# Small rows of w_up on four DMA loads of 8, 10, 12 and 14 engines

## The chip, the cores and the metric

The kernel runs on one core of a Trainium2 chip (trn2). The metric is the time of one execution in microseconds (us) of device time; lower is better. The first six runs of the kernel before agree within 0.3% (80.38 to 80.61 us). Some executions are over 1.5% slower than the fastest of their kernel; these are called slow and are left out of every comparison here, medians included. Two kernels, x8 and x14, were run once for their traces alone, so their state isn't known. In the profiles PE is TensorE (PEld its loads of weights), DVE is VectorE, ACT ScalarE, and SP the engine whose queue issues the loads. Because single traces matter in this study, each number says from which run it is.

## The reference, cut to what matters

One token is decoded: attention over a window of 4096 keys (part A) and a gated unit (part B), mixed by a gate. The change touches only `w_up`.

```python
def _B_ref(x, w_gate, w_up, w_down):          # x: 1x1x512, F = 1792
    g = jnp.einsum("bsd,df->bsf", x, w_gate)
    u = jnp.einsum("bsd,df->bsf", x, w_up)
    h = _sigmoid(g) * u
    return jnp.einsum("bsf,fd->bsd", h, w_down)
# ... a = attention(x, k_cache, v_cache, wq, wo)
return g * a + (1 - g) * b
```

All weights and caches together are 30.7 MB, each byte read once (the page of the kernel before counts 30.67 MB read), so the kernel is a stream of loads with the arithmetic beside it.

## The kernel before

All large loads are issued by SP in one order: wq, four of K (`kn`), w_gate, the main part of w_up, the small rows of w_up (`wx_sb`), four of V (`vv`), wo, w_down. A large load has 128 partitions and runs on all 16 DMA engines (busy share 1.00 of 16 from 60 to 69 us). A partition holds four rows of w_up; the last of the four, less its first 448 columns, is split off: 128 small rows of 1344 elements (2,688 bytes). They land in 64 partitions, in two slots `h`, by four loads of 32 rows:

```python
    wx_sb = const.tile([64, 2, FX], BF16, name="wx_sb")
    wx_v = B_w_up.rearrange("(h b j i c) f -> h b i j c f", h=2, b=2, j=4, i=8)[:, :, :, :, DC - 1, F - FX:F]
    for h in range(2):
        for b in range(2):
            dq.dma_start(wx_sb[32 * b:32 * b + 32, h, :], wx_v[h, b])
    # ... (cut) vv, wo, w_down
    spare = const.tile([1, 1], F32, name="spare")
    for _ in range(4):
        nc.vector.memset(spare[:], 0.0)
    # ... (cut) the same order of rows for x: xp, xx
    # in the second GLU, for the last quarter c == DC - 1 and j >= 1:
                    for h in range(2):
                        nc.tensor.matmul(g_out, lhsT=xx[:, h:h + 1].to_broadcast([64, 32]),
                                         rhs=wx_sb[:, h, (j - 1) * FQ:j * FQ], start=False, stop=(h == 1))
```

In the trace eight of 16 streams carry the rows, 16 each: no more than eight rows are under way at once, and each of the four loads counts eight completions. The other eight streams carry none of them. The trace has no engine numbers; the text calls the eight engines 0 to 7 and the others 8 to 15, as the description of the change does. It doesn't show either which partitions an engine writes. Where the rows land turns out to matter.

Of the kernel before, what the change touches and what calls it, by code (L numbers as in the profile page):

```python
# [12 lines left out]
BF16 = mybir.dt.bfloat16  # L13
F32 = mybir.dt.float32
# [3 lines left out]
def kernel(  # L18
# [14 lines left out]
    nc = tc.nc  # L33

    P = 128
    D = A_x.shape[-1]
    DC = D // P
# [8 lines left out]
    F = B_w_gate.shape[1]  # L46
# [3 lines left out]
    FQ = F // 4  # L50
# [11 lines left out]
    const = ctx.enter_context(tc.tile_pool(name="const", bufs=1))  # L62
# [7 lines left out]
    ps_m = ctx.enter_context(tc.tile_pool(name="ps_m", bufs=2, space=bass.MemoryType.PSUM))  # L70


    xr = const.tile([1, 2, D], BF16, name="xr")
# [3 lines left out]
    dq = nc.sync  # L77
# [11 lines left out]
    for a in range(HP):  # L89
# [7 lines left out]
    FX = 3 * FQ  # L97
    LM = DC * F - FX
    dq.dma_start(wu_sb[:].rearrange("p c f -> p (c f)")[:, 0:LM],
                 B_w_up.rearrange("(p c) f -> p (c f)", c=DC)[:, 0:LM])  # L100
    wx_sb = const.tile([64, 2, FX], BF16, name="wx_sb")
    wx_v = B_w_up.rearrange("(h b j i c) f -> h b i j c f", h=2, b=2, j=4, i=8)[:, :, :, :, DC - 1, F - FX:F]
    for h in range(2):
        for b in range(2):
            dq.dma_start(wx_sb[32 * b:32 * b + 32, h, :], wx_v[h, b])

    vv = []
    for a in range(HP):
# [16 lines left out]
    ident = const.tile([P, P], BF16, name="ident")  # L125
# [7 lines left out]
    nc.gpsimd.tensor_copy(permT[:].rearrange("p (k j) -> p k j", j=4),  # L133
                          ident[:].rearrange("p (j k) -> p k j", j=4))
    spare = const.tile([1, 1], F32, name="spare")
    for _ in range(4):
        nc.vector.memset(spare[:], 0.0)

    other = const.tile([2, HQ * 4 // R2, 2, REP], BF16, name="other")
# [7 lines left out]
    for c in range(DC):  # L147
        nc.tensor.matmul(xt_ps[:, c:c + 1], lhsT=xr[:, 0, c:D:DC], rhs=ident[0:1, 0:1],  # L148
                         start=True, stop=True, skip_group_check=True)
    xx_ps = ps_m.tile([64, 2], F32, name="xx_ps", tag="m")  # L150
    xp = const.tile([1, 2, 64], BF16, name="xp")
    for h in range(2):
        nc.vector.tensor_copy(xp[:, h, :].rearrange("o (b i j) -> o b i j", b=2, j=4),
                              xr[:, 0, :].rearrange("o (h b j i c) -> o h b i j c", h=2, b=2, j=4, i=8)[:, h, :, :, :, DC - 1])
        nc.tensor.matmul(xx_ps[:, h:h + 1], lhsT=xp[:, h, :], rhs=ident[0:1, 0:1],
                         start=True, stop=True, skip_group_check=True)
    xT = const.tile([P, DC], BF16, name="xT")
    nc.vector.tensor_copy(xT[:], xt_ps[:])
    xx = const.tile([64, 2], BF16, name="xx")
    nc.vector.tensor_copy(xx[:], xx_ps[:])  # L160


# [18 lines left out]
    for u in range(4):  # L181
        nc.tensor.matmul(S_ps[u // 2][:, u % 2, :], lhsT=other[:].rearrange("p o y u -> p (o y u)"),  # L182
                         rhs=ident[0:2, 0:2].rearrange("p (o y) -> p o y", o=1).to_broadcast([2, 256, 2]),
                         start=True, stop=False)
# [11 lines left out]
    for k in range(8):  # L196
        q_ps = ps_big.tile([P, 512], F32, name="q_ps", tag="b")
        ks = slice(k * 512, (k + 1) * 512)
        for c in range(DC):
            nc.tensor.matmul(q_ps[:], lhsT=xT[:, c:c + 1].to_broadcast([P, P]),  # L200
                             rhs=wq_sb[:, c, ks], start=(c == 0), stop=(c == DC - 1))
# [18 lines left out]
    for a in range(HP):  # L220
        for v in range(2):
            kT = kTs[a, v] if (a, v) in kTs else k_transpose(a, v)
            k_v = kT[:].rearrange("p (n dhi s t) -> p n dhi s t", n=KB, dhi=2, s=32)
            for dhi in range(2):
                for t in range(2):
                    for hb in range(2):
                        nc.tensor.matmul(S_ps[v][:, hb, :], lhsT=q_st[:, a, dhi, :, t],  # L227
                                         rhs=k_v[:, hb * 16:(hb + 1) * 16, dhi, :, t],
                                         start=False, stop=(a == HP - 1 and dhi == 1 and t == 1))
# [4 lines left out]
    def glu(w, wsb):  # L234
        for c in range(DC):
            for j in range(4):
                g_out = gu_ps[w][32 * j:32 * j + 32, 0:FQ]
                if w == 1 and c == DC - 1 and j >= 1:
                    for h in range(2):
                        nc.tensor.matmul(g_out, lhsT=xx[:, h:h + 1].to_broadcast([64, 32]),  # L240
                                         rhs=wx_sb[:, h, (j - 1) * FQ:j * FQ], start=False, stop=(h == 1))
                    continue
                nc.tensor.matmul(g_out, lhsT=xT[:, c:c + 1].to_broadcast([P, 32]),  # L243
                                 rhs=wsb[:, c, j * FQ:(j + 1) * FQ], start=(c == 0), stop=(c == DC - 1))


    pm2 = work.tile([P, 2], F32, name="pm2")
    for v in range(2):
        nc.vector.tensor_reduce(pm2[:, v:v + 1], S_ps[v][:].rearrange("p a b -> p (a b)"), axis=AX.X, op=ALU.max)  # L249
    pm = work.tile([P, 1], F32, name="pm")  # L250
    nc.vector.tensor_tensor(pm[:], pm2[:, 0:1], pm2[:, 1:2], op=ALU.max)
    glu(0, wg_sb)
    sge = work.tile([P, FQ], F32, name="sge")
    nc.scalar.activation(sge[:], gu_ps[0][:, 0:FQ], AF.Exp, scale=-1.0)  # L254
# [7 lines left out]
                     start=True, stop=True)  # L262
# [34 lines left out]
    for a in range(HP):  # L297
        for m in range(NP // 4):
            nc.tensor.matmul(pv_ps[32 * a:32 * a + 32, :, :],  # L299
                             lhsT=eT[:, a, 4 * m:4 * m + 4, :].rearrange("p n r -> p (n r)"),  # L300
                             rhs=vv[a][:, 4 * m:4 * m + 4, :],
                             start=(m == 0), stop=(m == NP // 4 - 1))
# [7 lines left out]


    glu(1, wu_sb)

    o_ps = ps_m.tile([P, HQ], F32, name="o_ps", tag="m")
# [59 lines left out]
```

## Time and profile before

| | before |
|---|---|
| time, median of the first 3 runs | 80.46 us (80.45 to 80.61) |
| span of the core in the profile | 78.7 us |
| share of the chain that ended last | DMA 93% |
| rate of the loads, 30 to 39 us | 426 GB/s |
| last completion count of w_down | 75.84 us |

The chain of waits tells what the end waited for, step by step. The windows tell how busy the 16 DMA engines are in a stretch. The records of single DMA packets, of which these views are made, hold start, length and size; where this document speaks of streams, every packet was linked to the one that ends where it starts, which gives one stream for each engine. "Landing" is the time at which an engine's count arrives at the semaphore of a load.

### The profile page before, as it was taken

What the parts mean: (1) busy time and instruction counts of PE and PEld (TensorE: products, weight loads), DVE (VectorE), ACT (ScalarE), POOL (GpSimd) and SP (SyncE); (2) the same over time, 40 slices, a digit from 0 to 9 for tenths busy, and PEclk for the clock granted to TensorE, in tenths of its full rate; (3) what the DMA queues carried; (4) which work ended last, traced back from release to release, by engine and by line L of the source; (5) the groups of instructions that cost most, each with busy time, mean ns of one, the idle gap of its engine ahead of it and who ended that gap; (6) DMA issues with size and microseconds to landing.
All of it is one profiled execution on the core that took longest, in us unless ns stands there. A gap on an engine that the chain in (4) does not pass through costs nothing.

```text
span 78.7 us, 798 instructions
## 1 busy us (share of the span) xinstructions
PE 52.5 (67%) x314; PEld 23.6 (30%) x314; DVE 38.8 (49%) x52; ACT 10.9 (14%) x20; POOL 3.3 (4%) x10
## 2 busy tenths in 40 slices
PE   0200094999905788898887307999996799567650
PEld 0200041344302333333332202344341345345420
DVE  1600920029869999999986349962000000690020
ACT  2400000247651000000002191000000002000010
POOL 7900000000000000000000000000000000000000
PEclk9999999999999999999999995699999999999997
DMA  7779799999999999999999999999999999999710
GB/s 184 300 316 533 316 483 391 408 425 458 441 408 416 425 474 416 386 437 417 438 410 426 441 416 441 408 433 441 416 433 433 424 425 433 416 391 409 290 42 1
DMA packets 2616, 30.71 MB, mean 390 GB/s; under 512 B 307, under 2 KB 438, under 8 KB 822
## 3 DMA queue, kind: packets, MB, share of 16 engines
q1 hardware_dynamic: 2608, 30.67, 92.9%
q8 instruction: 2, 0.03, 0.2%
q10 hardware_dynamic: 6, 0.00, 0.0%
HBM read 30.67 MB, written 0.00 MB: 390 GB/s over the span
## 4 chain that ended last, share of the span: by engine, by line
DMA 93%; SPq 2%; PE 1%; DVE 1%; issue 0%
DMA wd_sb<-in_B_w_down_dram 36%; DMA kn<-in_A_k_cache_dram 32%; DMA vv<-in_A_v_cache_dram 24%; SPq L84 2%; PE a_ps L290 1%; DVE res L341 1%; SPq L80 0%
## 5 line engine op out<-in xcount | busy, mean ns | idle before, releaser
L299 PE MATMUL pv_ps<-vv,eT 128*32 128x512 bf16 x64 | 15.9, 405 | 4.1 <-DVE eT L271 2.8
L227 PE MATMUL S_ps<-kT,qbig 128*128 128x512 bf16 x64 | 15.2, 378 | 5.0 <-DVE qbig L216 2.8
L188 DVE STREAM_TRANSPOSE kT<-kn 128x2048 f32<-128x2048 f32 x8 | 17.8, 2282 | 0.0
L227 PEld LDWEIGHTS <-qbig 128*128 128x128 bf16 x64 | 6.1, 97 | 14.1 <-issue 4.2
L299 PEld LDWEIGHTS <-eT 128*32 128x32 bf16 x64 | 6.2, 102 | 12.9 <-issue 4.2
L200 PE MATMUL q_ps<-wq_sb,xT 128*128 128x512 bf16 x32 | 8.8, 442 | 1.2 <-DMA wq_sb<-in_A_wq_dram 1.2
L318 DVE TENSOR_TENSOR oT<-o_ps,rb 128x32 bf16<-128x32 f32 x1 | 0.2, 191 | 13.5 <-PE o_ps L316 13.5
L205 DVE STREAM_TRANSPOSE qtT<-q_sb 128x512 f32<-128x512 f32 x4 | 2.7, 700 | 6.9 <-ACT q_sb L202 6.9
L182 PE MATMUL S_ps<-ident,other 2*128 2x512 bf16 x4 | 2.0, 611 | 5.8 <-DVE other L140 5.8
L202 ACT CAST q_sb<-q_ps 128x512 bf16<-128x512 f32 x8 | 4.7, 585 | 7.0 <-PE q_ps L200 7.0
L200 PEld LDWEIGHTS <-xT 128*128 128x128 bf16 x32 | 3.5, 111 | 6.8 <-issue 4.2
L290 PE MATMUL a_ps<-wo_sb,oY 128*1 128x256 bf16 x64 | 3.8, 272 | 1.5 <-DMA wo_sb<-in_A_wo_dram 1.2
L290 PEld LDWEIGHTS <-oY 128*1 128x1 bf16 x64 | 2.7, 83 | 3.1 <-issue 1.4
L271 DVE STREAM_TRANSPOSE eT<-e_sb 128x1024 bf16<-128x1024 bf16 x2 | 2.4, 1224 | 1.9 <-ACT e_sb L269 1.9
L254 ACT ACTIVATE sge<-gu_ps 128x448 f32<-128x448 f32 x1 | 0.5, 543 | 18.9 <-PE gu_ps L243 18.9
L309 ACT COPY pv_sb<-pv_ps 128x512 f32<-128x512 f32 x1 | 0.6, 585 | 17.7 <-PE pv_ps L299 17.7
L341 DVE CAST res<-a_ps 1x256 bf16<-1x256 f32 x1 | 0.4, 412 | 5.2 <-PE a_ps L290 5.2
L281 DVE RECIPROCAL sg<-sge 128x448 f32<-128x448 f32 x1 | 3.0, 2952 | 0.0
L165 DVE TENSOR_TENSOR gpr<-xr 1x512 f32<-1x512 bf16 x1 | 0.7, 679 | 4.6 <-DMA xr<-in_gate_w_dram 4.6
L249 DVE TENSOR_REDUCE pm<-S_ps 128x1 f32<-128x1024 f32 x2 | 2.4, 1208 | 0.9 <-PE S_ps L227 0.9
L290 PE MATMUL a_ps<-wd_sb,hT 128*1 128x256 bf16 x28 | 2.1, 271 | 0.8 <-DMA wd_sb<-in_B_w_down_dram 0.8
L148 PE MATMUL xt_ps<-ident,xr 1*128 1x1 bf16 x4 | 0.3, 165 | 3.5 <-POOL ident L126 3.5
(62 smaller groups left out, 31.0 us busy)
## 6 DMA issues: line engine op xcount, KB each, us to landing
kn<-in_A_k_cache_dram SPq DMA_DIRECT2D x4, 2048.0 KB, 27.2
vv<-in_A_v_cache_dram SPq DMA_DIRECT2D x4, 2048.0 KB, 19.1
wq_sb<-in_A_wq_dram SPq DMA_DIRECT2D x1, 4096.0 KB
wo_sb<-in_A_wo_dram SPq DMA_DIRECT2D x2, 2048.0 KB
wg_sb<-in_B_w_gate_dram SPq DMA_DIRECT2D x1, 1792.0 KB
wu_sb<-in_B_w_up_dram SPq DMA_DIRECT2D x1, 1456.0 KB
wd_sb<-in_B_w_down_dram SPq DMA_DIRECT2D x1, 1024.0 KB
wd_sb<-in_B_w_down_dram SPq DMA_DIRECT2D x1, 384.0 KB
```

Of the source, the lines that this page charges most:

```text
L84: dq.dma_start(t[:, n0:n1, :].rearrange("p n d -> p (n d)"), cache[0, 2 * a:2 * a + 2, SBASE:SBASE + W, :] .rearrange("y (x n) d -> x y n ...
L182: nc.tensor.matmul(S_ps[u // 2][:, u % 2, :], lhsT=other[:].rearrange("p o y u -> p (o y u)"), rhs=ident[0:2, 0:2].rearrange("p (o y) -> p ...
L188: nc.vector.transpose(t[:].bitcast(F32), kn[a][:, v * KB:(v + 1) * KB, :] .rearrange("p n d -> p (n d)").bitcast(F32))
L200: nc.tensor.matmul(q_ps[:], lhsT=xT[:, c:c + 1].to_broadcast([P, P]), rhs=wq_sb[:, c, ks], start=(c == 0), stop=(c == DC - 1))
L202: nc.scalar.copy(q_sb[:, ks], q_ps[:])
L205: nc.vector.transpose(qtT[:].bitcast(F32)[:, kq], q_sb[:].bitcast(F32)[:, kq])
L227: nc.tensor.matmul(S_ps[v][:, hb, :], lhsT=q_st[:, a, dhi, :, t], rhs=k_v[:, hb * 16:(hb + 1) * 16, dhi, :, t], start=False, stop=(a == HP ...
L249: nc.vector.tensor_reduce(pm2[:, v:v + 1], S_ps[v][:].rearrange("p a b -> p (a b)"), axis=AX.X, op=ALU.max)
L271: nc.vector.transpose(eT[:, :, v * KB:(v + 1) * KB, :].rearrange("p a n r -> p n a r"), e_sb[:, v, :].rearrange("p (n a r) -> p n a r", a= ...
L281: nc.vector.reciprocal(sg[:], sge[:])
L290: nc.tensor.matmul(a_ps[32 * i:32 * i + 1, i, 0:HN], lhsT=lhsT, rhs=rhs[:, i * HN:(i + 1) * HN], start=start, stop=stop)
L299: nc.tensor.matmul(pv_ps[32 * a:32 * a + 32, :, :], lhsT=eT[:, a, 4 * m:4 * m + 4, :].rearrange("p n r -> p (n r)"), rhs=vv[a][:, 4 * m:4 ...
```

## The change

Its intent, by the description that came with it: the rows spread over more engines, so that engines 8 to 15 carry 8 to 0 of them and engines 0 to 7 carry 12 instead of 16. The rows land in 128 partitions, one slot. That the kernel's 8, 10, 12 and 14 (`k` in the diff) would be the numbers of engines was an expectation; the trace of the kernel after tests it below.

```diff
-    wx_sb = const.tile([64, 2, FX], BF16, name="wx_sb")
-    wx_v = B_w_up.rearrange("(h b j i c) f -> h b i j c f", h=2, b=2, j=4, i=8)[:, :, :, :, DC - 1, F - FX:F]
-    for h in range(2):
-        for b in range(2):
-            dq.dma_start(wx_sb[32 * b:32 * b + 32, h, :], wx_v[h, b])
+    wx_sb = const.tile([P, FX], BF16, name="wx_sb")
+    WX_PARTS = []
+    for k, r in ((8, 4), (10, 3), (12, 2), (14, 3)):
+        e0 = sum(kk * rr for _, kk, rr in WX_PARTS)
+        WX_PARTS.append((e0, k, r))
+        dq.dma_start(wx_sb[e0:e0 + k * r, :], B_w_up[DC * e0:DC * (e0 + k * r), :]
+                     .rearrange("(j i c) f -> i j c f", j=r, i=k)[:, :, DC - 1, F - FX:F])
...
-    for _ in range(4):
+    for _ in range(2):
         nc.vector.memset(spare[:], 0.0)
... (xp is gathered by four copies instead of two, in the order of the rows; one xx matmul instead of two)
+                xc, rhs = xT[:, c:c + 1], wsb[:, c, j * FQ:(j + 1) * FQ]
                 if w == 1 and c == DC - 1 and j >= 1:
-                    for h in range(2):
-                        nc.tensor.matmul(g_out, lhsT=xx[:, h:h + 1].to_broadcast([64, 32]),
-                                         rhs=wx_sb[:, h, (j - 1) * FQ:j * FQ], start=False, stop=(h == 1))
-                    continue
... (cut)
+                    xc, rhs = xx[:], wx_sb[:, (j - 1) * FQ:j * FQ]
```

More of the change, by code (lines that the diff above doesn't have):

```diff
@@ L149 @@
                          start=True, stop=True, skip_group_check=True)
-    xx_ps = ps_m.tile([64, 2], F32, name="xx_ps", tag="m")
-    xp = const.tile([1, 2, 64], BF16, name="xp")
-    for h in range(2):
-        nc.vector.tensor_copy(xp[:, h, :].rearrange("o (b i j) -> o b i j", b=2, j=4),
-                              xr[:, 0, :].rearrange("o (h b j i c) -> o h b i j c", h=2, b=2, j=4, i=8)[:, h, :, :, :, DC - 1])
-        nc.tensor.matmul(xx_ps[:, h:h + 1], lhsT=xp[:, h, :], rhs=ident[0:1, 0:1],
-                         start=True, stop=True, skip_group_check=True)
+    xx_ps = ps_m.tile([P, 1], F32, name="xx_ps", tag="m")
+    xp = const.tile([1, P], BF16, name="xp")
+    for e0, k, r in WX_PARTS:
+        nc.vector.tensor_copy(xp[:, e0:e0 + k * r].rearrange("o (i j) -> o i j", i=k),
+                              xr[:, 0, DC * e0:DC * (e0 + k * r)].rearrange("o (j i c) -> o i j c", j=r, i=k)[:, :, :, DC - 1])
+    nc.tensor.matmul(xx_ps[:], lhsT=xp[:], rhs=ident[0:1, 0:1], start=True, stop=True)
     xT = const.tile([P, DC], BF16, name="xT")
     nc.vector.tensor_copy(xT[:], xt_ps[:])
-    xx = const.tile([64, 2], BF16, name="xx")
+    xx = const.tile([P, 1], BF16, name="xx")
     nc.vector.tensor_copy(xx[:], xx_ps[:])
@@ L237, in glu @@
                 g_out = gu_ps[w][32 * j:32 * j + 32, 0:FQ]
+                xc, rhs = xT[:, c:c + 1], wsb[:, c, j * FQ:(j + 1) * FQ]
                 if w == 1 and c == DC - 1 and j >= 1:
-                    for h in range(2):
-                        nc.tensor.matmul(g_out, lhsT=xx[:, h:h + 1].to_broadcast([64, 32]),
-                                         rhs=wx_sb[:, h, (j - 1) * FQ:j * FQ], start=False, stop=(h == 1))
-                    continue
-                nc.tensor.matmul(g_out, lhsT=xT[:, c:c + 1].to_broadcast([P, 32]),
-                                 rhs=wsb[:, c, j * FQ:(j + 1) * FQ], start=(c == 0), stop=(c == DC - 1))
+                    xc, rhs = xx[:], wx_sb[:, (j - 1) * FQ:j * FQ]
+                nc.tensor.matmul(g_out, lhsT=xc.to_broadcast([P, 32]), rhs=rhs,
+                                 start=(c == 0), stop=(c == DC - 1))
     pm2 = work.tile([P, 2], F32, name="pm2")
```

## The prediction

> **What bounds the kernel now.** I read the page's chain first. It says that the kernel is one long load:
>
> ```profile
> DMA 93%; SPq 2%; PE 1%; DVE 1%; issue 0%
> DMA wd_sb<-in_B_w_down_dram 36%; DMA kn<-in_A_k_cache_dram 32%; DMA vv<-in_A_v_cache_dram 24%; SPq L84 2%; PE a_ps L290 1%; DVE res L341 1%; SPq L80 0%
> ```
>
> The compute engines hold 1% each. The chain in order of time shows the end: the w_down load lands at 75.51 us, six matmuls and one copy follow.
>
> ```profile
> 46.84 28.67 DMA wd_sb<-in_B_w_down_dram
> 75.51 0.04 issue
> 75.55 0.66 PE a_ps L290 x6
> 76.20 0.40 DVE res L341
> ```
>
> So I ask which DMA engine brings the last piece of w_down. The windows of equal stretches answer half of it (columns: stretch, its length, busy us of PE, PEld, DVE, ACT, POOL, clock, DMA share of 16 engines, GB/s):
>
> ```profile
> 30.00:39.00 9.00, 7.85 (x35) 3.21 (x34) 9.00 (x5) 0.00 (x0) 0.00 (x0) 1.00 1.01 426
> ...
> 60.00:69.00 9.00, 6.91 (x60) 3.47 (x59) 1.40 (x4) 0.58 (x1) 0.00 (x0) 1.00 1.00 426
> ...
> 74.00:74.50 0.50, 0.50 (x12) 0.40 (x10) 0.00 (x0) 0.00 (x0) 0.00 (x0) 1.00 0.64 242
> 74.50:75.00 0.50, 0.50 (x13) 0.31 (x10) 0.00 (x0) 0.00 (x0) 0.00 (x0) 1.00 0.63 229
> 75.00:75.40 0.40, 0.36 (x6) 0.15 (x3) 0.00 (x0) 0.00 (x0) 0.00 (x0) 1.00 0.30 103
> ```
>
> All 16 engines are busy until 69 us, then a share of 0.63 is left, which is 10 of 16: six engines finish about 1.5 us before the other ten. The end is set by the engine with the most to carry, not by the sum of bytes. Why ten? The page's queues name the second kind of traffic:
>
> ```profile
> q1 hardware_dynamic: 2608, 30.67, 92.9%
> q8 instruction: 2, 0.03, 0.2%
> ```
>
> Two packets of instructions, of 16,384 bytes each. In the packet records of the trace I linked every packet to the one that ends where it starts; this gives 16 streams, one for each engine, though it doesn't give the engines' numbers. What the streams show:
> - A packet of 16,384 bytes takes 0.614 us in every stage (26.7 GB/s), alike on all engines. An engine runs at its own rate and never waits for another.
> - Eight streams carry the small rows (2,688 bytes, 16 each, four runs of four with a 4-byte completion after each). One row takes 0.104 us, one run 0.42 us, the four 1.68 us: for one such stream from 39.46 to 41.14 us. The other eight start on vv meanwhile.
> - The instruction packets start at 39.60 and 69.45 us, in two different streams, both of the eight without small rows. Each takes 1.06 and 1.10 us, and the data packet after it takes 1.11 us instead of 0.61 and 0.77 instead of 0.31. A fetch costs its engine 1.55 us.
>
> So the kernel before is balanced already: eight engines pay 1.68 us for small rows, two pay 1.55 us for a fetch, and six pay nothing and end early. At the end of wo, the streams with rows stand at 70.55 to 70.90 us, the one of the first fetch at 70.58, the others at 69.11 to 69.35; the one of these that the second fetch then hits stood at 69.14. From there to the end of w_down an undisturbed stream needs 4.48 us. Last packets are therefore at 75.03 to 75.38 (rows), 75.06 (first fetch), 69.14 + 4.48 + 1.56 = 75.18 (second), 73.6 to 73.8 (six free ones). The records' last packet indeed ends at 75.38; its completion counts 0.46 us later, at 75.84.
>
> [...]
>
> **The change, part by part.**
> *The loads.* (8,4), (10,3), (12,2), (14,3) are k and rows per engine.[...] Rows per engine: 0 to 7 have 4+3+2+3 = 12; 8 and 9 have 3+2+3 = 8; 10 and 11 have 2+3 = 5; 12 and 13 have 3; 14 and 15 none. The sum is 96+16+10+6 = 128, as before; 0.34 MB are moved and none removed. With 0.104 us for a row and 0.006 for a completion, engines 0 to 7 pay 12 x 0.104 + 4 x 0.006 = 1.27 us instead of 1.68, so they end 0.41 us earlier, at 74.62 to 74.97. Engines 8 to 15 pay 0.85, 0.85, 0.53, 0.53, 0.32, 0.32, 0, 0.
> An engine without a fetch then ends at 73.8 + 0.85 = 74.65 at most and isn't last. What matters is the two with a fetch: they stood at 75.06 and 75.18, and keep that or add their rows. The last engine moves from 75.38 to 75.18 (no rows: -0.20 us), to about 75.5 (three rows: +0.1), 75.7 (five: +0.3) or 76.0 (eight: +0.6).
> *Issue.* Four loads remain, each 0.68 to 0.82 us on SP's queue. The last is issued by 23.4 us, while the engines reach them at 39.5 us. Nothing of this is on the path.
> *PE.* In the second GLU three matmuls of 128 rows replace six of 64. The six stand from 65.69 to about 66.25 us, so about 0.28 us less work, and one transposition of x replaces two at the start. PE then waits 1.22 us for wo and 0.8 us for w_down, so this gain is hidden.[...]
> *DVE.* Four small copies for xp instead of two, two dummy memsets instead of four: the count is kept, and DVE waits 4.6 us for gate_w there. Nothing.
>
> **The rivals.**
> (a) *The fetches hit engines 14 and 15, or others without rows.* For it: the gradient looks drawn for this, and both fetches fell on the upper half. Then the last engine gains only 0.2 us, since the fetch engine becomes the bound: 80.25 us.
> (b) *A fetch hits engine 8 or 9.* For it: nothing in the trace says which of the upper eight it is. Against it: the design. The time would be 80.46 + 0.6 = 81.05 us.
> (c) *The full gain of 0.41 us.* It needs fetches that cost nothing, or that end before; the streams at 75.06 and 75.18 speak against it. 80.05 us.
> (d) *A fetch moves to an engine with 12 rows*[...]: 1.27 + 1.55 against 1.68, so +1.1 us, 81.6 us. Against it: four runs of before within 0.22 us of each other suggest that the engine is fixed[...].
> (e) *A wait for PE takes over.* Against: it is ahead of the loads from 66 us on.
>
> **Range and chances.** I can't see the engine numbers, so I weigh by hand: no rows on the worse fetch engine 0.35 (-0.2 us), three rows 0.25 (+0.1), five 0.2 (+0.3), eight 0.2 (+0.6); together +0.13 us. I take 80.5 us. Streams differ in phase by 0.35 us from their start on, which shifts who is last by 0.1 to 0.2 us; with cases (a) to (b) this gives 80.1 to 81.1 us. 2% is 1.6 us; faster by that is out of reach, as all 16 engines' mean end is (8 x 75.2 + 2 x 75.1 + 6 x 73.7)/16 = 74.6, only 0.8 us before the last. Slower by it needs (d) and more.
>
> **What would show it right or wrong.** In the packet records of the changed kernel the streams should carry 12, 8, 5, 3 and 0 rows of 2,688 bytes on eight, two, two, two and two engines, which also tells the number of the fetch's engine up to a pair. The rows' streams should end vv 0.41 us earlier against the free ones. In the last half microsecond before the end the DMA share should fall to one or two sixteenths (0.06 to 0.13) instead of ten, because only fetch engines are left; the last landing of w_down should sit 1.55 us plus rows after a free engine's. It is wrong if the last streams are again those of engines 0 to 7, if a fetch costs other than 1.55 us, or if k comes out otherwise (all rows of a load on one or two engines would cost whole microseconds).

## The result, and the profile after

| | before | after |
|---|---|---|
| median of 6 runs | 80.46 us (80.38 to 80.61) | 81.88 us (81.18 to 83.03), two of them slow |
| fast runs | all six, median 80.46 | 81.18, 81.70, 81.78, 81.98, median 81.74 |
| ratio, fast runs | | 1.0147 (95%: 1.0106 to 1.0187) |

A ratio is the mean time of one kernel's fast runs over that of the other's fast runs of the same rounds, so it isn't quite the ratio of the medians. The change costs 1.5%; the prediction, 80.5 us in a range of 80.1 to 81.1, missed it.

First what came out as worked out. The page's queues of the kernel after (packets, MB, share of 16 engines):

```profile
q1 hardware_dynamic: 2620, 30.67, 91.9%
q8 instruction: 2, 0.03, 0.2%
```

The load queue has 12 packets more than before and the same bytes. That is 8+10+12+14 = 44 completions for the rows instead of 4 x 8 = 32, and at their semaphores the four loads count 8, 10, 12 and 14: they do run on so many engines. And again there are two instruction packets. At the end of the loads, in equal stretches of the kernel after (DMA share and GB/s are the last two columns):

```profile
75.50:76.00 0.50, 0.50 (x10) 0.34 (x6) 0.00 (x0) 0.00 (x0) 0.00 (x0) 0.50 0.13 47
76.00:76.50 0.50, 0.50 (x12) 0.37 (x10) 0.00 (x0) 0.00 (x0) 0.00 (x0) 0.87 0.06 20
```

A share of 0.13, then 0.06: two engines, then one, as the prediction had it for the streams that were hit by a fetch. But they are at it half a microsecond to a microsecond later than was worked out. What was missed lies around 40 us. One stretch from 39 to 43.5 us, in which the rows are read and the first V load begins, before and after:

```profile
39.00:43.50 4.50, 3.54 (x28) 1.25 (x26) 3.49 (x4) 0.54 (x1) 0.00 (x0) 1.00 1.03 426
```

```profile
39.00:43.50 4.50, 4.21 (x32) 1.69 (x30) 3.62 (x3) 0.00 (x0) 0.00 (x0) 1.00 1.03 345
```

The reader should look at the last two columns. Busy share 1.03 in both (the share comes from the packets' lengths, so it can pass 1), but 426 GB/s before and 345 after: the engines are occupied all the time and move a fifth less. (426 - 345)/426 x 4.5 us = 0.86 us are lost, by all 16 engines together. The packet records say the same. Before, all 128 rows take 107 to 112 ns. After, the rows take about 107 ns up to 40.05 us, and from then on, as the third load begins, up to 294 ns (61 of the 128 take over 115 ns); the V packets beside them take up to 1.20 us instead of 0.614. Even the two streams without rows land their first V load at 45.99 and 46.10 us, where an unburdened stream of the kernel before did so at 45.05 to 45.27.

The second part is at the end. The chain of waits in order of time, kernel after:

```profile
42.50 30.09 DMA wo_sb<-in_A_wo_dram
72.58 0.04 issue
72.62 5.15 PE a_ps L289 x60
77.77 0.40 DVE res L340
```

Before, six matmuls followed the last landing. Here the chain leaves the loads at wo and follows PE through its last 60 matmuls. The windows say why; PEclk, third column from the right, is the granted clock of TensorE (before, then after):

```profile
72.70:76.10 3.40, 2.60 (x40) 1.53 (x34) 0.00 (x0) 0.00 (x0) 0.00 (x0) 1.00 0.56 211
```

```profile
72.70:76.10 3.40, 3.40 (x34) 2.21 (x35) 0.00 (x0) 0.00 (x0) 0.00 (x0) 0.50 0.76 295
```

In this execution TensorE was granted half its clock (0.50) from 72.71 to 76.13 us, and PE was busy all through it (3.40 of 3.40 us). The last landing was at 76.87 us, and the output's DMA was issued 1.38 us later; before it was 0.84 us. So the profiled execution's 1.58 us (span 80.32 against 78.74) divide into 76.87 - 75.84 = 1.03 us of later landing and 1.38 - 0.84 = 0.54 us of half-clock tail. Only the first part is in every trace of the kernel after. Its second trace, below, has a full clock in the tail and 81.18 us.

### The profile page after: what moved, and what is told of

Same layout as the page of the kernel before. It is cut to its first block, busy times and chain, and to the rows that moved or that the text cites. A ratio compares the mean times of both kernels' runs of the same rounds, so it can differ in the third digit from the quotient of the medians.

```text
span 80.3 us, 790 instructions
## 1 busy us (share of the span) xinstructions
PE 54.5 (68%) x310; PEld 24.6 (31%) x310; DVE 38.8 (48%) x52; ACT 10.9 (14%) x20; POOL 3.3 (4%) x10
## 4 chain that ended last, share of the span: by engine, by line
DMA 83%; PE 6%; SPq 6%; issue 1%; DVE 0%
DMA wu_sb<-in_B_w_up_dram 46%; DMA wo_sb<-in_A_wo_dram 37%; PE a_ps L289 6%; SPq L84 4%; SPq L94 1%; SPq L117 1%; DVE res L340 0%; SPq L80 0%
## 5 line engine op out<-in xcount | busy, mean ns | idle before, releaser
L228 PE MATMUL S_ps<-kT,qbig 128*128 128x512 bf16 x64 | 16.3, 404 | 3.9 <-DVE qbig L217 2.8
L201 PE MATMUL q_ps<-wq_sb,xT 128*128 128x512 bf16 x32 | 9.4, 466 | 1.6 <-DMA wq_sb<-in_A_wq_dram 1.6
L289 PE MATMUL a_ps<-wo_sb,oY 128*1 128x256 bf16 x64 | 5.4, 343 | 2.5 <-DMA wo_sb<-in_A_wo_dram 2.2
L289 PEld LDWEIGHTS <-oY 128*1 128x1 bf16 x64 | 3.4, 102 | 4.8 <-issue 2.4
L253 ACT ACTIVATE sge<-gu_ps 128x448 f32<-128x448 f32 x1 | 0.5, 544 | 18.9 <-PE gu_ps L242 18.9
L183 PEld LDWEIGHTS <-other 2*128 2x128 bf16 x4 | 0.6, 158 | 6.2 <-DVE other L142 5.9
```

Source lines behind the costliest of these rows:

```text
L183: nc.tensor.matmul(S_ps[u // 2][:, u % 2, :], lhsT=other[:].rearrange("p o y u -> p (o y u)"), rhs=ident[0:2, 0:2].rearrange("p (o y) -> p ...
L201: nc.tensor.matmul(q_ps[:], lhsT=xT[:, c:c + 1].to_broadcast([P, P]), rhs=wq_sb[:, c, ks], start=(c == 0), stop=(c == DC - 1))
L228: nc.tensor.matmul(S_ps[v][:, hb, :], lhsT=q_st[:, a, dhi, :, t], rhs=k_v[:, hb * 16:(hb + 1) * 16, dhi, :, t], start=False, stop=(a == HP ...
L289: nc.tensor.matmul(a_ps[32 * i:32 * i + 1, i, 0:HN], lhsT=lhsT, rhs=rhs[:, i * HN:(i + 1) * HN], start=start, stop=stop)
```

## The experiments

The theory after the first look: **P**, the place: rows are slow because of the partitions in which they land, and the jam spreads to other streams. Behind it stood an assumption of the author about which engine writes which partitions, and that engines slow each other where they write side by side. No trace here shows that; the runs show only what each choice of partitions and of rows for each engine took. Rivals: **R**, the new order of reading rows from memory; **F**, the fetch of instructions, which in the profiled run began at 40.14 us, within 0.1 us of the stall; **G**, rows on more than eight engines stall wherever they land.

All results in one table; the first kernel's profiled trace and the second trace of it (in the row "before") agree within 0.1 us. "Rows" is the sum of the lengths of the 128 row packets, "rate" the stretch 39 to 43.5 us, "landing" the last count of w_down in the trace, "closing" the time from the output's DMA issue to the end of the span.

| kernel | fast runs, us | ratio to before | rows, us | rate, GB/s | landing, us | closing, us |
|---|---|---|---|---|---|---|
| before (traces: first, x8) | 80.31 to 80.71 | 1 | 13.7, 13.7 | 426, 430 | 75.84, 75.91 | 2.05, 2.06 |
| after (traces: first, x4, x11, x14) | 81.11 to 82.18 | 1.015, 1.015, 1.016 | 18.1, 17.5, 18.9, 18.0 | 345, 342, 321, 331 | 76.87, 76.64, 77.63, 76.55 | 2.07, 2.06, 2.06, 2.06 |
| x1_upper | 81.91 to 82.03 | 1.020 | 24.2 | 274 | 77.42 | 2.06 |
| x2_even16 | 81.03 to 81.39 | 1.010 | 13.7 | 431 | 76.33 | 2.24 |
| x3_lower | 81.77 to 82.18 | 1.019 | 22.2 | 294 | 77.20 | 2.29 |
| x5_pairs | 81.17 to 81.76 | 1.013 | 19.5 | 337 | 76.95 | 2.18 |
| x6_shift4 | 80.14 to 80.98 | 1.002 | 14.2 | 403 | 75.57 | 2.29 |
| x7_ten | 80.67 to 81.39 | 1.009 | 15.7 | 405 | 76.28 | 2.02 |
| x9_aligned | 80.95 to 81.39 | 1.009 | 13.7 | 430 | 76.25 | 2.34 |
| x10_best | 80.56 to 81.29 | 1.005 | 13.7 | 416 | 75.70 | 2.28 |
| x12_best64 | 80.23 to 80.64 | 0.9988 | 13.7 | 433 | 75.92 | 2.05 |
| x13_before65 | 80.74 to 81.08 | 1.005 | 13.7 | 426 | 75.93 | 2.28 |

### x1_upper: the old loads into the other half of the partitions

```diff
-            dq.dma_start(wx_sb[32 * b:32 * b + 32, h, :], wx_v[h, b])
+            dq.dma_start(wx_sb[64 + 32 * b:96 + 32 * b, h, :], wx_v[h, b])
... (tile of 128 partitions; xx_ps, xx and the matmuls use partitions 64 to 127)
```

> The kernel before, its four loads of eight engines unchanged, but the rows land in partitions 64 to 127 instead of 0 to 63. Theory P[...]: the rows' packets take well over 107 ns, all engines are held up by 0.9 to 1.7 us around 40 to 42 us as in the changed kernel, the time is 81.3 to 82.2 us. Theory R (reads: the order in which rows are read from memory, or the uneven k, causes the stall) and theory F (the instruction fetch falling among the small rows causes it): nothing changes, 80.4 to 80.6 us, rows at 107 ns.

The same engines read the same rows in the same order; only the partitions differ. The window of its trace:

```profile
39.00:43.50 4.50, 4.21 (x28) 1.76 (x31) 3.73 (x3) 0.00 (x0) 0.00 (x0) 1.00 1.04 274
```

274 GB/s: (426 - 274)/426 x 4.5 = 1.6 us lost. The median row takes 207 ns, and the time is 81.99 us (median of the fast runs), as theory P had it (81.3 to 82.2). The fetch began at 41.24 us, long after the rows had become slow. R and F expected no change and fall as causes of this much; where the rows land is enough to make a stall larger than that of the change.

### x2_even16: one load on 16 engines, one row for each partition

```diff
-    for k, r in ((8, 4), (10, 3), (12, 2), (14, 3)):
-        ...
+    WX_PARTS = [(0, P, 1)]
+    wx_v = B_w_up.rearrange("(p c) f -> p c f", c=DC)[:, DC - 1, F - FX:F]
+    dq.dma_start(wx_sb[:], wx_v)
... (five dummy memsets instead of two, as xp needs one copy instead of four)
```

> The changed kernel with one load of 128 rows in natural order, 8 rows on each of 16 engines[...]. All theories of the prediction: every engine pays 8 rows, 0.83 us, the fetch engines end 0.83 us later than in the kernel before, so 80.46 + 0.6 = 81.1 us. Theory P: no stall, rows at 107 ns and vv packets at 0.614 us throughout, 81.0 to 81.2 us. Theory R and F, by which reading the rows on many engines or a fetch among them stalls everything: a stall of 0.9 us on top, about 82 us.

```profile
39.00:43.50 4.50, 3.57 (x29) 1.29 (x28) 3.48 (x4) 0.54 (x1) 0.00 (x0) 1.00 1.04 431
```

No stall, rows at 107 to 114 ns, though rows are now on all 16 engines. The median is 81.23 us, where the prediction's sum (a fetch plus eight rows on one engine) gives 81.1. That the two agree to 0.13 us is in part luck: the landing moved by 0.42 to 0.49 us against the two traces of before, where the sum has 0.6, and the closing is 0.18 us longer, which the sum doesn't have. So the sum holds to about 0.2 us in this run without slow rows.

### x3_lower: the changed loads into partitions 0 to 65

```diff
-    wx_sb = const.tile([P, FX], BF16, name="wx_sb")
+    wx_sb = const.tile([66, 2, FX], BF16, name="wx_sb")
-        dq.dma_start(wx_sb[e0:e0 + k * r, :], B_w_up[DC * e0:DC * (e0 + k * r), :]
+        h, d0 = (0, e0) if e0 < 62 else (1, e0 - 62)
+        dq.dma_start(wx_sb[d0:d0 + k * r, h, :], B_w_up[DC * e0:DC * (e0 + k * r), :]
... (two matmuls of 62 and 66 rows where the changed kernel has one of 128)
```

> The changed kernel's four loads with the same k, rows, sources and order, but landing in partitions 0 to 65 (loads one and two in 0 to 61, three and four beside them in 0 to 65). Theory P: engines 14 and 15[...] are no longer held up and end their first vv load about 0.9 us earlier than in the changed kernel;[...] the time lies between, 80.6 to 81.6 us. Theory R and F: the same stall on all engines as in the changed kernel, 81.2 to 82 us.

```profile
39.00:43.50 4.50, 3.57 (x30) 1.29 (x27) 3.40 (x4) 0.54 (x1) 0.00 (x0) 1.00 1.02 294
```

This one missed in part. The time, 81.95 us, lies above the 80.6 to 81.6 that P had named, and the two earliest streams land their first V load at 46.39 and 46.42 us, later than in the changed kernel (45.99 and 46.10) and not 0.9 us earlier. With the rows in partitions 0 to 65 the jam is larger (294 GB/s) than with the same loads in 0 to 127 (321 to 345 in four traces). And it isn't confined to the streams with rows, though P had expected the two without rows to go free. P needs this correction: streams without rows are held up too. F loses again: the fetch began at 39.44 us, while rows stay at 107 ns up to 40.1 us, where the third load begins. R, which expected this much, isn't refuted by this run. x1 shows that a stall needs no new order of reading, and x9 below reads rows in an order of the same form as the change's without a stall.

### x4_after: the changed kernel again

> The changed kernel again, for a second trace and for its spread. The stall at 40 to 42 us belongs to the change if it is there again, with all 16 streams late by about 0.9 us at the end of the first vv load, engines 14 and 15 (no rows) among them; the fetch again on streams with 5 and 3 rows if its engine is fixed. Time 81.2 to 82.1 us in fast runs. If the half-clock windows of TensorE fall elsewhere, the end follows the last landing (about 77 us) and the time is near 81.2; if one covers the tail, near 82.

```profile
39.00:43.50 4.50, 3.70 (x29) 1.31 (x26) 3.58 (x4) 0.47 (x1) 0.00 (x0) 1.00 1.02 342
```

The stall is there again, 342 GB/s. The chain's end in this trace is that of the kernel before, only later:

```profile
47.20 29.14 DMA wd_sb<-in_B_w_down_dram
76.34 0.04 issue
76.38 0.62 PE a_ps L289 x6
77.00 0.40 DVE res L340
```

TensorE has its full clock in the tail, and the execution took 81.18 us. The landing, 76.64 us, is 0.80 us after the first trace of before, and so is the span (79.54 against 78.74). This is the cost of the change with nothing else on top. The fast runs of this kernel are 81.18, 81.21, 82.00 and 82.13 us.

### x5_pairs: two loads of 64 rows within the lower half

```diff
-    wx_v = B_w_up.rearrange("(h b j i c) f -> h b i j c f", h=2, b=2, j=4, i=8)[:, :, :, :, DC - 1, F - FX:F]
+    wx_v = B_w_up.rearrange("(h j i c) f -> h i j c f", h=2, j=8, i=8)[:, :, :, DC - 1, F - FX:F]
-            dq.dma_start(wx_sb[32 * b:32 * b + 32, h, :], wx_v[h, b])
+        dq.dma_start(wx_sb[:, h, :], wx_v[h])
... (xp in the same order)
```

> The kernel before with the same 16 rows on each of engines 0 to 7, in partitions 0 to 63, but as two loads of 64 rows instead of four of 32[...]. Theory P[...]: rows take about 200 ns, the row phase grows from 1.7 to about 3.3 us and the time by 1 to 1.7 us, to 81.4 to 82.1 us. Rival P2[...]: rows 107 ns, 80.4 to 80.6 us.

```profile
39.00:43.50 4.50, 4.02 (x30) 1.49 (x28) 3.61 (x3) 0.14 (x1) 0.00 (x0) 1.00 1.04 337
```

Eight engines carry the same number of rows into the same 64 partitions, eight rows each in one load instead of four each in two. That costs 1.3% (81.63 us, the median of the fast runs): the landing is 1.04 to 1.11 us later than in the traces of before, and the closing 0.13 us longer. The median row takes 147 ns and the slowest 235, less than the 200 that was expected for the median. The rival P2, by which only rows that land in partitions 64 to 127 hurt, falls. That engines meet in pairs there was the author's assumption and isn't shown. And again the streams without rows suffer: they land their third V load at 55.74 to 55.97 us, against 54.84 to 55.07 in the kernel before. By which path the jam spreads, no run here shows.

### x6_shift4: the old loads moved by four partitions

```diff
-            dq.dma_start(wx_sb[32 * b:32 * b + 32, h, :], wx_v[h, b])
+            dq.dma_start(wx_sb[4:36, 2 * h + b, :], wx_v[h, b])
... (four slots of 36 partitions, the first four zero; gpr in bf16 to make room)
```

> The kernel before with its four loads moved from partitions 0 to 31 and 32 to 63 to partitions 4 to 35 (four slots beside each other)[...]. Theory P[...]: rows 107 ns, hardly a stall, 80.4 to 80.8 us. Rival P3[...]: rows near 200 ns and 81.4 to 82.1 us.

```profile
39.00:43.50 4.50, 4.16 (x28) 1.72 (x31) 3.61 (x3) 0.00 (x0) 0.00 (x0) 1.00 1.03 403
```

The median row is at 107 ns and the rate at 403 GB/s, the ratio is 1.002 (0.993 to 1.011). Other partitions than the old ones are no harm by themselves, and the rival P3, by which any move makes rows slow, falls. Some rows still take up to 209 ns; why, this trace doesn't show. The fast runs scatter (80.14, 80.49, 80.98 us), so this run bears no finer reading.

### x7_ten: an attempt with rows on ten engines

```diff
-    for k, r in ((8, 4), (10, 3), (12, 2), (14, 3)):
+    for k, r in ((8, 4), (10, 3), (8, 4), (10, 3), (4, 1)):
... (destination as in x3_lower)
```

> An attempt to beat both: rows only on engines 0 to 9, by loads of 8x4, 10x3, 8x4, 10x3 and 4x1 rows in partitions 0 to 65: engines 0 to 3 carry 15, 4 to 7 carry 14, 8 and 9 carry 6, and 10 to 15 none, since in the changed kernel the fetches hit streams with 5 and 3 rows.[...] rows' streams end 0.1 to 0.2 us earlier, 80.25 to 80.45 us. If it isn't: rows over 107 ns and 80.6 to 81.5 us.

It doesn't beat the kernel before: 81.19 us in the median of the fast runs. Row packets sum to 15.7 us instead of 13.7, the rate is 405 GB/s: of the two cases it is the one in which rows take over 107 ns. The second load of the changed kernel has ten engines with three rows each too, and its first trace showed no slow rows there; why not stays open. It isn't free in every trace: in x11 and x14 76 and 70 rows take over 115 ns, while the third and fourth loads hold only 66.

### x8_before: the kernel before, once more

> The kernel before, unchanged, for a second trace: rows at 107 ns, fetches on two streams without rows, last landing of w_down near 75.8 us, 80.3 to 80.6 us. If TensorE has two or three half-clock windows instead of one, it shows whether the tail after 71 us is hit and what that costs: by the changed kernel's trace up to 0.6 us.

80.48 us, rows at 107 to 112 ns, 430 GB/s, last landing 75.91 us, and once more seven streams early and nine late after the first V load (44.91 to 45.27 and 46.38 to 46.89 us). It had full clock in the tail, so what a half-clock window would do to this kernel's tail isn't shown.

### x9_aligned: the intent with four rows for each engine

Here every load gives each engine four rows, as the kernel before does, and the loads of ten and of 14 engines begin at partition 32. That engines then don't meet where they write was the author's assumption.

```diff
-    for k, r in ((8, 4), (10, 3), (12, 2), (14, 3)):
+    for h, d0, k, r, st in ((0, 0, 8, 4, 1), (0, 32, 10, 4, 1), (1, 32, 14, 4, 1)):
+        d1 = d0 + k * r * st
+        dq.dma_start(wx_sb[d0:d1:st, h, :], ...
... (two slots; unused partitions 0 to 31 of the second are zeroed; xp and xx to match)
```

> The changed kernel's intent with nearly its gradient[...]: loads of 8, 10 and 14 engines with four rows each, the last two starting at partition 32[...]. Rows per engine: 12 on 0 to 7, 8 on 8 and 9, 4 on 10 to 13, none on 14 and 15. Theory P: rows 107 ns, no stall, and the prediction's own sum holds: the fetch streams (4 rows) end last, at 75.1 to 75.2 + 0.42 us, the time is 80.5 to 80.8 us, no more than 0.3 above the kernel before. Rival G (rows on more than eight engines stall whatever they write): a stall of 0.8 us and 81.2 to 82 us as in the changed kernel.

```profile
39.00:43.50 4.50, 3.48 (x28) 1.23 (x26) 3.44 (x4) 0.54 (x1) 0.00 (x0) 1.00 1.04 430
```

Rows on 14 engines with nearly the gradient of the change, every row at 107 to 112 ns, and 430 GB/s: the stall is gone, and rival G falls. R falls too, since the rows are read in an order of the same form as the change's. The time, 81.25 us, is above the expected 80.5 to 80.8, though. The trace has two reasons. The two fetch streams, both with four rows, land last, at 76.16 and 76.25 us; that is 0.34 to 0.41 us after the two traces of before, where 0.2 to 0.3 was worked out. And the closing takes 2.34 us instead of 2.05, which the next runs take up.

### x10_best, x12_best64 and x13_before65: beating both, and a dummy memset

x10 has loads of 8x4, 10x4, 10x4 and 8x2 rows that begin at partitions 0, 32, 32 and 0: 14 rows on engines 0 to 7, 8 on engines 8 and 9, none on the fetch streams.

```diff
-    for k, r in ((8, 4), (10, 3), (12, 2), (14, 3)):
+    for h, d0, k, r, st in ((0, 0, 8, 4, 1), (0, 32, 10, 4, 1), (1, 32, 10, 4, 1), (1, 0, 8, 2, 2)):
... (as x9_aligned)
```

> Rows on engines 0 to 9 only[...]: loads of 8x4, 10x4, 10x4 and 8x2 rows, 14 rows on engines 0 to 7, 8 on 8 and 9, none on the fetch streams if these are among 10 to 13 as in the changed kernel. Theory P and the prediction's sum: rows' streams end 0.2 us earlier, level with the fetch streams: 80.2 to 80.4 us, 0.1 to 0.2 below the kernel before. Rival G: 81 us or more. If the fetch falls on 8 or 9: 80.46 + 0.6 us.

The last landing came at 75.70 us, 0.14 and 0.21 us before the two traces of before, as worked out, and yet the time (fast runs 80.56 to 81.29 us, median 81.05) wasn't below it. In the trace the closing barrier waited for VectorE's last drain: 124 ns long and 0.4 us late. In each trace with 65 VectorE instructions (x3, x6, x9, x10) this drain takes 124 to 142 ns, in those with 64 it takes 19 ns. It isn't a matter of more instructions, though: x7 has 66, a drain of 24 ns and a closing of 2.02 us. Nor is it all: x2 and x5 have 64 and a drain of 19 ns, and their closings are 2.24 and 2.18 us; they also issue fewer loads, and what lengthens theirs wasn't tested. So the count was changed alone, down in x10 and up in the kernel before:

```diff
# x12_best64, against x10_best                    # x13_before65, against before
-    for _ in range(2):                           -    for _ in range(4):
+    for _ in range(1):                           +    for _ in range(5):
         nc.vector.memset(spare[:], 0.0)                   nc.vector.memset(spare[:], 0.0)
```

> x10 with one dummy memset fewer, so that VectorE again has the 64 instructions of the kernel before. If their number sets the closing barrier: VectorE's last drain takes some 19 ns instead of 124 to 142, the time from the output's DMA to the end is 2.05 us instead of 2.28, and fast runs are at 80.2 to 80.4 us (x10: 80.56 and 80.61 at best), just below the kernel before. If not: as x10.

> The kernel before with a fifth dummy memset, 65 instructions on VectorE and nothing else changed. If their number sets the closing barrier: 2.28 us from the output's DMA to the end, fast runs at 80.65 to 80.75 us, 0.23 above the kernel before. If not: 80.4 to 80.6 us.

One memset of one element makes the kernel before slower: 80.88 against 80.44 us, ratio 1.005 (1.0034 to 1.0066). Of these 0.4 us the trace shows 0.23 in the closing (2.28 against 2.05), with a last drain of 144 ns; the rest stays open. With 64 again, the aligned version runs at 80.35 us in the median against 80.44:

```profile
39.00:43.50 4.50, 4.10 (x31) 1.50 (x28) 3.61 (x3) 0.07 (x1) 0.00 (x0) 1.00 1.05 433
```

Its ratio, 0.9988 (0.9971 to 1.0006), is clearly better than the change's, but whether it beats the kernel before can't be said; its trace landed at 75.92 us, no earlier than before's. The old split already was within some 0.1 us of what moving rows can give.

### x11_after and x14_after: where the changed kernel's scatter comes from

> The changed kernel a third time, for the tail. In all traces the last landing of w_down should be at 76.6 to 76.9 us. If TensorE's half-clock window falls on 72.5 to 76 us, the last 60 matmuls end after the landings and the time is 81.7 to 82.1 us; if not, 81.2 us.

> The changed kernel a fourth time. The stall of all streams is there again, first vv load at 45.9 to 46.1 us on the earliest two streams. If the fetches always hit the same engines: streams with 5 and 3 rows again, last landing 76.6 to 76.9 us. If they wander: another stream, and a last landing up to 77.6 us.

Both traces have the stall (321 and 331 GB/s) and full clock in the tail. x14 landed at 76.55 us, in the expected range, and took 81.11 us. x11 missed its range: it landed at 77.63 us and took 82.18 us without a half-clock window in the tail. By the order in which streams had ended their first V load, the second fetch hit the third of 16 in the first trace and in x4, the second in x14, and about the twelfth in x11, a stream that ended late anyway. So the fast runs' spread, 81.1 to 82.2 us, has two sources in these traces: which stream a fetch hits, and in one trace a half-clock window in the tail. How often each occurs isn't known; four traces don't tell.

## Why the prediction was wrong, point by point

- **"An engine runs at its own rate and never waits for another"**: this is the step that failed. It was read off the kernel before, where the packets of rows took 107 to 112 ns and nothing contradicted it. The change gave the rows other partitions, and the prediction counted rows for each engine without asking where they land. In the changed kernel the row phase loses 0.9 to 1.1 us on all engines (345, 342, 321 and 331 GB/s instead of 426). x1 ties it to the place (274 GB/s with the old loads in partitions 64 to 127), x5 has it in the old partitions with eight rows for each engine in a load instead of four (337), and x6 shows that not every move does it (403). x9 shows that rows on up to 14 engines run without the stall with other partitions and four rows for each engine (430). What happens at the partitions isn't shown.
- **"Engines 0 to 7 end 0.41 us earlier"**: they didn't. In x14 most streams' last landings lie between 75.9 and 76.45 us, while the kernel before ended its ten late ones between 75.52 and 75.84. The sum itself holds where no rows are slow, to about 0.2 us, by the landings of x2, x9 and x10.
- **k, rows and completions** were right: 8, 10, 12 and 14 completions, 12 packets more on the queue, streams with fewer rows among the sixteen, the same bytes.
- **A fetch costs its engine 1.55 us, and fetch streams end last**: the order was right. The last stretches show two engines and then one (shares of 0.13 and 0.06). In the kernel after, the two packets of instructions took 1.28 and 1.11 us, against 1.06 and 1.10 before. For which engine they are isn't shown. With the fetch on streams of few rows, the gain of 0.41 us couldn't have shown anyway, as rival (a) said.
- **"The engine is fixed"**, said against rival (d): not so in the changed kernel. In three of four traces the second fetch hit one of the three streams that had ended their first V load earliest, in the fourth about the twelfth of 16, and that one landed 0.8 to 1.1 us later (77.63 us against 76.55 to 76.87).
- **PE is ahead of the loads** (against rival (e)): true in three of four traces. In the profiled one a half-clock window cost 0.54 us. PE had less in hand, because wo lands later. The waits of PE for wo, before and then after:

```profile
PE a_ps L290 <- DMA wo_sb<-in_A_wo_dram: 1.2, 1, 1.2
```

```profile
PE a_ps L289 <- DMA wo_sb<-in_A_wo_dram: 2.2, 1, 2.2
```

  The second fetch began at 70.44 us. Before, its stream had finished wo at 69.14 us, just ahead of it; now the stalled stream was still at wo, whose landing moved from 71.34 to 72.58 us.
- **VectorE: "the count is kept ... Nothing"**: the result was right, the reason not seen. Keeping the count mattered: one instruction more costs 0.4 us in x13.
- **Rival (c), rows to spare for a better split**: the most that alignment and a better split gave is a median of 80.35 against 80.44 us, which the interval of the ratio (0.9971 to 1.0006) doesn't tell apart.

## What to carry to other kernels

When a kernel is bound by DMA and loads are steered to certain engines, count rows for each engine and also write down in which partitions each load lands and how many rows it gives an engine. Here rows took 107 to 114 ns in a load of 128 partitions with one row each (x2) and in loads that begin at partition 0 or 32 and give each engine four rows, or two in every second partition (x9, x10, x12); other choices cost up to 1.6 us of all engines' time (x1). In these runs the base partition and the number of rows for each engine in a load made the difference. One case doesn't fit as simply, the second load of the change (see x7). A view of busy share doesn't show such a jam, since the share stayed at 1.03; the rate does (426 GB/s before, 345 after). And a rate that was the same on all engines in one trace is a property of that traffic, not of the engines: a V packet that took 0.614 us before took up to 1.20 us after.
